# Lightning attention and a snake MLP in one kernel: squares taken off VectorE, matmuls without a reader, and a new program order

## Chip, core and metric

The kernel runs on one core of one Trainium2 chip. The metric is the device time of one launch in microseconds. Before the change the median of three runs is 239.01 us (238.47, 239.01 and 242.13).

The engines go by short names: PE is TensorE, DVE is VectorE, ACT is ScalarE, POOL is GpSimd, SP is SyncE, which here only issues transfers.

## The reference, cut to what matters

```python
# q, k, v: (4 batches, 8 heads, 768 positions, 64); lam: (8,)
for b in range(12):                                   # blocks of 64 positions
    intra = (qb @ kb.T * Dmask) @ vb                  # Dmask[i, j] = lam**(i-j) for i >= j
    inter = (qb * lam**(pos+1)) @ kv_state
    out[block] = intra + inter
    kv_state = lam**64 * kv_state + (kb * lam**(63-pos)).T @ vb

x = out.transpose(0, 2, 1, 3).reshape(3072, 512)      # tokens x model
h = x @ w_in                                          # 512 -> 2048
g = h + sin(alpha * h)**2 / (alpha + 1e-9)            # "snake"
y = g @ w_out                                         # 2048 -> 512
```

Inputs and output are float32. The kernel multiplies in bfloat16 and accumulates in float32.

## The kernel before

The work is cut into units and groups. A unit `u` is one batch, a window of 256 positions and four of the eight heads (24 units). Four units make a group `g` of 512 tokens (6 groups). Units run through attention, groups through the two layers of the MLP; both are interleaved.

Every engine takes its instructions strictly in the order of one string, `ORDER`. An item is `kind.indices:engine[:bank]`; the engine letters are T (PE), V (DVE), A (ACT), G (POOL) and S (SP), and the bank says which PSUM bank a matmul group uses. What an item waits for on other engines comes from its data, by semaphores. The kinds:

| kind | what it does |
|---|---|
| ld | load q, k or v of a unit (256 KB) |
| wi, wo | load a quarter of w_in or w_out, cast to bf16 by the transfer; issued by POOL |
| sq, sk, cv | scale q by lam^(pos+1), k by its reciprocal; cast v |
| tq, tk, tcq, tck | transpose q or k on PE, and copy the result out of PSUM |
| tdq, tdk | the same transposes by DMA (from unit 8 on) |
| s, m | scores on PE, and the causal mask on DVE |
| k, kc, a, n | k-v product on PE, its copy, the decayed state, the next state |
| o, x | attention output on PE, and its copy to bf16, the MLP's input |
| f1a, f1 | first layer, 128 of the 2048 columns: four matmuls of 512 tokens (f1a and f1: two halves of 256) |
| sin, sqr, stt | sine, its square, and h + square / alpha |
| f2 | second layer: a quarter of the sum for 128 tokens: four matmuls |
| oc, st | copy out of PSUM, store |
| lt, ltc | the last 128 tokens, in two halves of the columns |

A stretch of the order string, where the first squares stand:

```
... sin.0.0:A sin.0.1:A sin.0.2:A sqr.0.0:V f1a.0.3:T:5 f1.0.3:T kc.5:A tck.5:V sqr.0.1:G wi.2:G cv.6:V
k.6:T sqr.0.2:A sin.0.3:A tk.6:T:0 stt.0.0:V wi.3:G sq.7:V kc.6:A sqr.0.3:A tq.7:T:3 tck.6:A ...
```

The parts of the program that the change and the steps below touch (`...` marks cuts):

```python
    N0 = 28
    ...
    BANK = ("h0", "h1", "h2", "h3", "s0", "s1")
    def psum(shape, dtype, name, bank):
        return ps.tile(shape, dtype, name=name, tag=BANK[bank], bufs=1)
    ...
    def load_w_in(j, **_):                       # one quarter; POOL issues it
        w = DFF // WCH
        ld = nc.gpsimd.dma_start(out=w_in_sb[:, :, j * w:(j + 1) * w], in_=...)
        if j == 0:
            after(ld, loads[GATE])               # GATE = (3, 0): q of unit 3
    ...
    def scaled(u, j, name, bufs, tab, eng):      # sq, sk
        eng.tensor_tensor(out=t[:], in0=stage[u, j]..., in1=tab..., op=ALU.mult)
    ...
    def kv_decayed(u, c, eng, **_):              # a
        if prev is not None:
            eng.tensor_tensor(out=t[:], in0=x, in1=prev[:], op=ALU.add)      # kvx
        eng.tensor_tensor(out=kvbd[u, c][:], in0=x..., in1=LBD..., op=ALU.mult)
    ...
    def f1_part(g, f, bs):
        for c in range(NDC):                     # 4
            mlp[0] = nc.tensor.matmul(out=hps[g, f]..., lhsT=w_in_sb[:, c, f * P:(f + 1) * P],
                                      rhs=xt[g][:, c, bs]..., start=..., stop=...)
    def sine(g, f, **_):
        nc.scalar.activation(out=s1[g, f][:], in_=hps[g, f][:], func=ACTF.Sin,
                             scale=alpha_sb[:, f:f + 1])
    def square(g, f, eng, **_):
        if eng is nc.scalar:
            nc.scalar.activation(out=s2[g, f][:], in_=x[:], func=ACTF.Square)
        else:
            eng.tensor_tensor(out=s2[g, f][:], in0=x[:], in1=x[:], op=ALU.mult)
    def snake(g, f, **_):                        # stt; frees the PSUM bank of hps
        nc.vector.scalar_tensor_tensor(out=gall[g][:, f, :], in0=s2.pop((g, f))[:],
                                       scalar=r_sb[:, f:f + 1], in1=hps.pop((g, f))[:],
                                       op0=ALU.mult, op1=ALU.add)
    ...
    bz = ps.tile([P, 2 * P], FP32, name="bz", tag="h1", bufs=1)
    for _ in range(N0):                          # matmuls without a reader, at the start
        nc.tensor.matmul(out=bz[:], lhsT=zeros[:, :P], rhs=zeros[:], start=True, stop=True)
    ...
    for item in ORDER.split():
        name, eng, *bank = item.split(":")
        kind, *ix = name.split(".")
        DO[kind](*map(int, ix), eng=ENG[eng], bank=int(bank[0]) if bank else None)
```

Attention's PSUM tiles are `sp` in the banks s0 and s1 and `okv`, of which there is one.

Of the kernel before, what the change touches and what calls it, by code (L numbers as in the profile page):

```python
# [11 lines left out]
FP32 = mybir.dt.float32  # L12
# [6 lines left out]
ld.0.0:S ld.0.1:S sk.0:V sq.0:G tq.0:T:3 tk.0:T:0 ld.0.2:S ld.1.0:S ld.1.1:S ld.1.2:S ld.2.0:S  # L19
ld.2.1:S ld.2.2:S sk.1:G cv.0:V ld.3.0:S ld.3.1:S ld.3.2:S ld.4.0:S ld.4.1:S ld.4.2:S ld.5.0:S k.0:T  # L20
cv.1:G tcq.0:A tck.0:A tables:V sq.1:V s.0:T m.0.0:V kc.0:A m.0.1:V a.0.0:G k.1:T kc.1:A sq.2:V
sk.2:G sq.3:G sk.3:G ld.5.1:S ld.5.2:S ld.6.0:S ld.6.1:S ld.6.2:S ld.7.0:S ld.7.1:S ld.7.2:S
ld.8.0:S ld.8.1:S ld.8.2:S ld.9.0:S cv.2:A ld.9.1:S ld.9.2:S ld.10.0:S ld.10.1:S ld.10.2:S n.0.0:G
tq.1:T:3 tcq.1:V tk.1:T:2 tq.2:T:1 tck.1:V s.1:T m.1.0:V m.1.1:V tq.3:T:0 cv.3:A tcq.2:A o.0:T
tk.2:T:3 tck.2:A tk.3:T:2 a.1.0:V n.1.0:G s.2:T sq.4:V sk.4:V x.0.0:A o.1:T tck.3:V m.2.0:V m.2.1:V
x.1.0:A tcq.3:A k.2:T kc.2:V k.3:T cv.4:G sq.5:V kc.3:A tq.4:T:2 cv.5:A wi.0:G a.2.0:V s.3:T
tq.5:T:1 k.4:T kc.4:V tk.4:T:3 m.3.0:V m.3.1:V tck.4:A a.3.0:G sk.5:G o.2:T x.2.0:A a.4.0:V tcq.4:V
o.3:T a.1.1:V tcq.5:A x.3.0:A sq.6:G s.4:T tq.6:T:0 f1a.0.0:T:1 x.3.1:V tcq.6:A m.4.0:V n.4.0:V
sk.6:V f1.0.0:T tk.5:T:3 f1a.0.1:T:2 f1.0.1:T f1a.0.2:T:4 f1.0.2:T wi.1:G m.4.1:V n.1.1:G k.5:T
sin.0.0:A sin.0.1:A sin.0.2:A sqr.0.0:V f1a.0.3:T:5 f1.0.3:T kc.5:A tck.5:V sqr.0.1:G wi.2:G cv.6:V  # L30
k.6:T sqr.0.2:A sin.0.3:A tk.6:T:0 stt.0.0:V wi.3:G sq.7:V kc.6:A sqr.0.3:A tq.7:T:3 tck.6:A
stt.0.1:V stt.0.2:V sk.7:G stt.0.3:V f1.0.4:T:1 sin.0.4:A f1.0.5:T:2 n.3.0:V a.6.0:V tcq.7:A
sin.0.5:A o.4:T x.4.0:A s.5:T sqr.0.4:V stt.0.4:V tk.7:T:0 n.6.0:G f1.0.6:T:3 m.5.0:V m.5.1:V
tck.7:A cv.7:G k.7:T a.5.0:G sqr.0.5:G f1.0.7:T:1 sin.0.6:A kc.7:V s.6:T stt.0.5:V sqr.0.6:A
stt.0.6:V m.6.0:V m.6.1:V o.5:T f1.0.8:T:0 sin.0.7:A sqr.0.7:A sin.0.8:A f1.0.9:T:2 wo.0:G stt.0.7:V
a.7.0:G sqr.0.8:G f1.0.10:T:3 stt.0.8:V x.5.0:A wo.1:G sin.0.9:A sqr.0.9:A stt.0.9:V s.7:T o.6:T
m.7.0:V m.7.1:V f1.0.11:T:1 f1.0.12:T:0 sin.0.10:A sqr.0.10:A stt.0.10:V sin.0.11:A sqr.0.11:V
stt.0.11:V f1.0.13:T:2 f1.0.14:T:4 sin.0.12:A sqr.0.12:G n.5.0:V stt.0.12:V x.6.0:A sin.0.13:A o.7:T
sin.0.14:A x.7.0:A sqr.0.13:A sqr.0.14:A f1a.1.0:T:5 f1.0.15:T:3 f1.1.0:T sin.0.15:A a.0.1:G
stt.0.13:V sin.1.0:A stt.0.14:V sqr.0.15:V stt.0.15:V sk.8:G f1a.1.1:T:1 sqr.1.0:G stt.1.0:V  # L40
f1.1.1:T sin.1.1:A f1a.1.2:T:0 f1.1.2:T f1a.1.3:T:4 f1.1.3:T f1.1.4:T:2 sqr.1.1:G sin.1.2:A
sqr.1.2:V cv.8:G stt.1.1:V sin.1.3:A sqr.1.3:A sin.1.4:A stt.1.2:V f1.1.5:T:3 sin.1.5:A sqr.1.4:A
f1.1.6:T:5 sqr.1.5:A stt.1.3:V stt.1.4:V sin.1.6:A a.3.1:V k.8:T stt.1.5:V ld.11.0:S f1.1.7:T:1
cv.9:G sqr.1.6:A f1.1.8:T:4 f1.1.9:T:0 sin.1.7:A sqr.1.7:V n.0.1:V f1.1.10:T:2 sin.1.8:A sin.1.9:A
sqr.1.8:A sin.1.10:A stt.1.6:V wo.2:G stt.1.7:V sq.8:G f2.0.1.0:T:3 n.2.0:G a.2.1:G wo.3:G stt.1.8:V
f2.0.1.1:T f1.1.11:T:1 tdq.8:S ld.11.1:S ld.11.2:S cv.10:A sqr.1.9:A kc.8:A a.8.0:V sin.1.11:A
f2.0.1.2:T sk.9:G k.9:T sq.9:G n.3.1:V sq.10:G f2.0.0.0:T:4 sqr.1.10:V f2.0.0.1:T f2.0.0.2:T
f2.0.0.3:T oc.0.0:A kc.9:V tdk.8:S n.8.0:G sk.10:G sqr.1.11:V stt.1.9:V f2.0.2.0:T:0 f2.0.2.1:T
stt.1.10:V sq.11:G cv.11:A a.9.0:V a.5.1:V s.8:T n.2.1:G ld.12.0:S tdq.9:S tdk.9:S tdq.10:S m.8.0:V
tdq.11:S k.10:T f2.0.1.3:T m.8.1:V f1.1.12:T:2 n.7.0:V tdk.10:S kc.10:V s.9:T sk.11:G k.11:T  # L50
a.10.0:V sin.1.12:A st.0.0.0:S ld.12.1:S oc.0.1:V a.6.1:G f2.0.2.2:T f2.0.2.3:T a.7.1:G m.9.0:V
m.9.1:V kc.11:A sq.12:G o.8:T ld.12.2:S oc.0.2:V x.8.0:A s.10:T cv.12:A sqr.1.12:V m.10.0:V
f1.1.13:T:3 m.10.1:V n.9.0:G n.6.1:G n.5.1:V tdk.11:S o.9:T sin.1.13:A x.9.0:A f2.0.3.0:T:0
f2.0.3.1:T ld.13.0:S stt.1.11:V ld.13.1:S ld.13.2:S ld.14.0:S ld.14.1:S ld.14.2:S ld.15.0:S s.11:T
ld.15.1:S tdq.12:S n.10.0:V a.11.0:G sk.12:G o.10:T x.10.0:A sq.13:G stt.1.12:V f2.0.3.2:T tdq.13:S
f2.0.3.3:T sqr.1.13:G m.11.0:V m.11.1:V sq.14:G tdk.12:S sq.15:G stt.1.13:V ld.15.2:S ld.16.0:S
ld.16.1:S o.11:T x.11.0:V ld.16.2:S oc.0.3:V cv.13:A f1.1.14:T:1 f1.1.15:T:4 k.12:T sin.1.14:A
f1.2.0:T:5 f1.2.1:T:2 sqr.1.14:V stt.1.14:V sin.1.15:A sin.2.0:A a.4.1:G sk.13:G sqr.1.15:V
stt.1.15:V sqr.2.0:A stt.2.0:V sin.2.1:A f1.2.2:T:0 sin.2.2:A n.4.1:G a.9.1:G f1.2.3:T:3 n.11.0:V
sk.14:G n.7.1:G a.8.1:G f1.2.4:T:1 sin.2.3:A sqr.2.1:V stt.2.1:V sqr.2.2:A stt.2.2:V sin.2.4:A  # L60
sqr.2.3:V sqr.2.4:A tdq.14:S st.0.0.1:S tdq.15:S f1.2.5:T:4 kc.12:V f1.2.6:T:5 f1.2.7:T:0 sin.2.5:A
sin.2.6:A sin.2.7:A sqr.2.5:A stt.2.3:V stt.2.4:V sqr.2.6:V stt.2.5:V st.0.3.0:S tdk.13:S sqr.2.7:G
st.0.2.0:S f1.2.8:T:2 k.13:T f1.2.9:T:3 kc.13:A cv.14:A sin.2.8:A sqr.2.8:A stt.2.6:V f2.1.0.0:T:1
f2.1.0.1:T s.12:T sk.15:G stt.2.7:V k.14:T f1.2.10:T:0 tdk.14:S ld.17.0:S ld.17.1:S sin.2.9:A
f2.1.0.2:T sk.16:G n.8.1:G sqr.2.9:A kc.14:A m.12.0:V m.12.1:V a.12.0:G cv.15:G o.12:T ld.17.2:S
tdk.15:S n.9.1:G stt.2.8:V stt.2.9:V x.12.0:A s.13:T f1.2.11:T:2 a.10.1:G ld.18.0:S m.13.0:V
m.13.1:V k.15:T f2.1.0.3:T a.13.0:V kc.15:A oc.1.0:A s.14:T o.13:T sq.16:G sin.2.10:A cv.16:A
x.13.0:A f2.1.1.0:T:3 a.14.0:V m.14.0:V tdq.16:S st.0.1.0:S st.0.1.1:S sq.17:G sq.18:G tdq.17:S
m.14.1:V f1.2.12:T:1 s.15:T sin.2.11:A cv.17:A sqr.2.10:G a.15.0:V m.15.0:V stt.2.10:V o.14:T
x.14.0:A sin.2.12:A sqr.2.11:V sqr.2.12:V f2.1.1.1:T stt.2.11:V stt.2.12:V f2.1.1.2:T k.16:T  # L70
f1.2.13:T:4 sin.2.13:A n.12.0:V m.15.1:V f2.1.1.3:T sqr.2.13:V f1.2.14:T:0 sk.17:G stt.2.13:V
sin.2.14:A f1.2.15:T:2 tdk.16:S ld.18.1:S kc.16:V n.15.0:G sk.18:G s.16:T m.16.0:V o.15:T x.15.0:V
f2.1.2.0:T:1 oc.1.1:A f2.1.2.1:T sqr.2.14:V stt.2.14:V f1.3.0:T:3 sin.2.15:A sin.3.0:A ld.18.2:S
tdk.17:S f2.1.2.2:T k.17:T kc.17:A n.13.0:V f1.3.1:T:0 ld.19.0:S st.0.3.1:S a.11.1:G sqr.2.15:G
sin.3.1:A stt.2.15:V sqr.3.0:A m.16.1:V cv.18:G k.18:T s.17:T tdq.18:S tdk.18:S ld.19.1:S ld.19.2:S
ld.20.0:S st.0.2.1:S f2.1.2.3:T f2.1.3.0:T:2 f2.1.3.1:T cv.19:A sqr.3.1:G m.17.0:V stt.3.0:V
oc.1.2:V st.1.2.0:S sq.19:G tdq.19:S n.10.1:V m.17.1:V f1.3.2:T:3 f1.3.3:T:1 f2.1.3.2:T f2.1.3.3:T
kc.18:V a.16.0:V sk.19:G a.18.0:G n.11.1:G s.18:T stt.3.1:V o.16:T sin.3.2:A sqr.3.2:A m.18.0:V
sin.3.3:A oc.1.3:A sqr.3.3:A f1.3.4:T:0 x.16.0:V stt.3.2:V a.12.1:V sin.3.4:A sqr.3.4:A f1.3.5:T:4
stt.3.3:V ld.20.1:S ld.20.2:S ld.21.0:S ld.21.1:S stt.3.4:V a.17.0:V m.18.1:V f2.2.0.0:T:2  # L80
f2.2.0.1:T tdk.19:S f1.3.6:T:3 sin.3.5:A f1.3.7:T:0 k.19:T f1.3.8:T:5 sqr.3.5:V sin.3.6:A sqr.3.6:V
sin.3.7:A sqr.3.7:A stt.3.5:V sin.3.8:A st.1.0.0:S st.1.0.1:S st.1.3.0:S ld.21.2:S stt.3.6:V kc.19:V
st.1.1.0:S sqr.3.8:A ld.22.0:S ld.22.1:S f1.3.9:T:1 sin.3.9:A ld.22.2:S f2.2.0.2:T stt.3.7:V
f1.3.10:T:3 f1.3.11:T:0 stt.3.8:V sin.3.10:A st.1.3.1:S n.14.0:G sq.20:G s.19:T o.17:T a.14.1:V
f2.2.0.3:T sqr.3.9:G stt.3.9:V x.17.0:A f1.3.12:T:1 sqr.3.10:V o.18:T sk.20:G sk.21:G sin.3.11:A
oc.2.0:A a.19.0:V stt.3.10:V sq.21:G cv.20:G cv.21:G m.19.0:V f2.2.1.0:T:3 f1.3.13:T:2 f2.2.1.1:T
cv.22:G sin.3.12:A tdq.20:S st.2.0.0:S tdq.21:S sqr.3.11:V x.18.0:V sqr.3.12:A sin.3.13:A sqr.3.13:G
m.19.1:V stt.3.11:V stt.3.12:V a.15.1:G a.13.1:G n.15.1:V stt.3.13:V o.19:T f1.3.14:T:5 f1.3.15:T:4
f2.2.1.2:T x.19.0:A sin.3.14:A sin.3.15:A sq.22:G f2.2.1.3:T f2.2.2.0:T:0 f2.2.2.1:T f2.2.2.2:T
ld.23.0:S st.1.1.1:S sqr.3.14:G sqr.3.15:A st.2.0.1:S n.14.1:G tdk.20:S f1.4.0:T:1 sin.4.0:A  # L90
# [32 lines left out]
def kernel(  # L123
# [11 lines left out]
    nc = tc.nc  # L135
    P = nc.NUM_PARTITIONS
# [452 lines left out]
```

## Time and profile before

| | |
|---|---|
| time, median of three runs | 239.01 us |
| time of the profiled run | 243.51 us |
| its span, first to last instruction | 241.7 us |
| TensorE clock granted, mean | 0.932 |
| transfers | 33.92 MB, mean 140 GB/s |
| stores at the end: PE's last matmul to the end of the span | 236.2 to 241.7 us |

How to read it: the page's first part gives each engine's busy time, its share of the span and its instructions. The second part cuts the span into forty slices of 6.04 us; a digit is the busy share in tenths, and PEclk is the clock that TensorE was granted, in tenths of full speed. A table by stretch gives the same for stretches of one's choosing, in microseconds. A line of the waits reads: engine and line that waited, what it waited for, us in total, times, longest. A line in order of time reads: start, duration, engine, source line, operation, output and inputs. L452 is the first layer's matmul, L472 the sine, L481 the square on DVE or POOL, L479 the square on ACT, L486 the snake, L495 the second layer's matmul, L276 the scaling, L253 and L261 the loads of w_in and w_out. Matmuls overlap in the pipeline and their ends are modelled, so a busy PE does not mean that it works at its peak.

### The profile page before, as it was taken

Reading aid. Unit: us, or ns where it says so; the run is one execution under the profiler, and the core shown is the slowest. Engines: PE = TensorE matmul, PEld = TensorE weight load, DVE = VectorE, ACT = ScalarE, POOL = GpSimd, SP = SyncE. Lnnn points to the kernel's source line nnn. Section 1 sums busy time; section 2 is a strip of 40 time slices with the busy share of each in tenths; the row PEclk is TensorE's granted clock in tenths of the full one; section 3 lists DMA queues with packets and bytes.
Section 4 is the critical chain, followed back from the end, with each engine's and each line's share of the span. In section 5 each row is a group of like instructions: output and inputs, shape, how many; then the busy total and the mean of one; then the engine's idle time right before and its main releaser. Section 6 shows DMA issues by size and latency. Waiting matters only on the chain.

```text
span 241.7 us, 5272 instructions
## 1 busy us (share of the span) xinstructions
PE 216.5 (90%) x2049; PEld 112.1 (46%) x2077; DVE 166.2 (69%) x290; ACT 119.1 (49%) x207; POOL 110.3 (46%) x148
## 2 busy tenths in 40 slices
PE   8487599699959999998999997999999999999990
PEld 5354375246414554454444444444445444444460
DVE  2977758598996998989967999347676645664100
ACT  2244349489841336956535565427763255544010
POOL 5756237338955667797339046941532101111000
PEclk9955569799979999999999999999999999999998
DMA  5999979990898999984863994404811200305314
GB/s 147 292 290 248 247 198 198 221 170 5 131 163 161 191 291 200 193 195 93 215 178 90 224 232 108 90 0 91 188 32 43 60 8 0 87 1 113 87 23 109
DMA packets 63850, 33.92 MB, mean 140 GB/s; under 512 B 19648, under 2 KB 60880, under 8 KB 63824
## 3 DMA queue, kind: packets, MB, share of 16 engines
q1 hardware_dynamic: 59344, 29.31, 54.0%
q0 software_dynamic: 4224, 4.19, 11.0%
q8 instruction: 16, 0.26, 0.5%
q10 hardware_dynamic: 256, 0.08, 0.1%
q14 instruction: 10, 0.08, 0.1%
HBM read 27.28 MB, written 6.29 MB: 139 GB/s over the span
## 4 chain that ended last, share of the span: by engine, by line
PE 65%; DVE 9%; DMA 7%; issue 6%; ACT 4%; SPq 4%; POOL 2%; ACTq 0%; POOLq 0%
PE ops L495 31%; PE hps L452 25%; SPq L243 4%; DMA w_in_sb<-in_moe_w_in_dram 4%; DMA st_k<-in_k_dram 3%; ACT s L472 2%; DVE gall L486 2%; PE sp L344 2%; DVE s L481 2%; PE okv L429 2%; PE okv L420 2%; PE okv L375 1%; PE ops L518 1%; DVE ST L354 1%; DVE kvbd L397 1%
## 5 line engine op out<-in xcount | busy, mean ns | idle before, releaser
L452 PE MATMUL hps<-xt,w_in_sb 128*128 128x512 bf16 (+1 forms) x403 | 94.4, 379 | 7.4 <-DMA w_in_sb<-in_moe_w_in_dram 3.7
L472 ACT ACTIVATE s<-hps,alpha_sb 128x512 bf16<-128x512 f32 x96 | 64.9, 688 | 59.5 <-PE hps L452 50.5
L495 PE MATMUL ops<-w_out_sb,gall 128*128 128x512 bf16 x353 | 84.7, 381 | 2.8 <-DVE gall L486 1.3
L486 DVE SCALAR_TENSOR_TENSOR gall<-s,r_sb,hps 128x512 bf16<-128x512 bf16 x96 | 69.6, 742 | 22.7 <-POOL s L481 12.4
L481 POOL TENSOR_TENSOR s<-s 128x512 bf16<-128x512 bf16 x25 | 26.3, 1054 | 81.5 <-ACT s L472 72.1
L452 PEld LDWEIGHTS <-w_in_sb 128*128 128x128 bf16 x416 | 40.4, 102 | 48.0 <-issue 6.1
L495 PEld LDWEIGHTS <-gall 128*128 128x128 bf16 x368 | 34.9, 98 | 42.9 <-issue 2.4
L354 DVE TENSOR_TENSOR ST<-sp,mask 128x512 bf16<-128x512 f32 x48 | 31.3, 682 | 9.9 <-PE sp L344 9.7
L481 DVE TENSOR_TENSOR s<-s 128x512 bf16<-128x512 bf16 x33 | 20.5, 621 | 11.0 <-ACT s L472 10.9
L276 POOL TENSOR_TENSOR KD<-st_k,R 128x512 bf16<-128x512 f32 x21 | 23.0, 1101 | 5.4 <-PE hps L452 3.9
L479 ACT ACTIVATE s<-s 128x512 bf16<-128x512 bf16 x38 | 23.6, 630 | 0.9 <-DVE gall L486 0.3
L276 POOL TENSOR_TENSOR QL<-st_q,E 128x512 bf16<-128x512 f32 x19 | 20.4, 1075 | 4.2 <-DMA st_q<-in_q_dram 3.8
L267 ACT COPY ob<-ops 128x512 f32<-128x512 f32 (+1 forms) x16 | 8.9, 557 | 24.8 <-PE ops L495 22.3
L267 ACT CAST xt<-okv 128x512 bf16<-128x512 f32 (+1 forms) x18 | 10.4, 577 | 14.1 <-PE okv L429 14.1
L344 PE MATMUL sp<-QT 64*64 64x128 bf16 x384 | 11.5, 235 | 1.7 <-DVE ST L354 0.7
L397 DVE TENSOR_TENSOR kvbd<-kvx,LBD 128x256 bf16<-128x256 f32 x17 | 11.4, 669 | 0.6
L344 PEld LDWEIGHTS <-QT 64*64 64x64 bf16 x384 | 7.5, 115 | 8.3 <-issue 6.2
L429 PE MATMUL okv<-ST,VB 64*64 64x128 bf16 x384 | 10.9, 237 | 0.0
L375 PE MATMUL okv<-VB,KD 64*64 64x64 bf16 x320 | 7.9, 205 | 3.2 <-POOL VB L269 1.5
L269 DVE COPY ob<-ops 128x512 f32<-128x512 f32 x9 | 6.1, 683 | 6.6 <-PE ops L495 6.6
L267 ACT COPY QT<-pt 128x512 bf16<-128x512 bf16 x11 | 6.5, 598 | 7.6 <-PE pt L303 7.6
L375 PEld LDWEIGHTS <-KD 64*64 64x64 bf16 x320 | 5.7, 115 | 9.6 <-issue 7.3
(59 smaller groups left out, 147.3 us busy)
## 6 DMA issues: line engine op xcount, KB each, us to landing
st_q<-in_q_dram SPq DMA_DIRECT2D x24, 256.0 KB, 5.2
st_k<-in_k_dram SPq DMA_DIRECT2D x24, 256.0 KB, 5.0
st_v<-in_v_dram SPq DMA_DIRECT2D x24, 256.0 KB, 5.2
out_dram<-ob SPq DMA_DIRECT2D x46, 128.0 KB, 2.4
w_in_sb<-in_moe_w_in_dram POOLq DMA_DIRECT2D x4, 512.0 KB, 9.6
w_out_sb<-in_moe_w_out_dram POOLq DMA_DIRECT2D x4, 512.0 KB, 8.5
QT<-QL SPq DMA_TRANSPOSE x16, 3.1
QT<-KD SPq DMA_TRANSPOSE x16, 3.2
```

The source lines that it names most:

```text
L267: nc.scalar.copy(out=out, in_=in_)
L276: eng.tensor_tensor(out=t[:], in0=stage[u, j][:].rearrange("p h two e -> p two h e"), in1=tab[:, :, hh * HH:(hh + 1) * HH].unsqueeze(3).to ...
L344: nc.tensor.matmul(out=sp[hd][half[c], par, hp, :], lhsT=QT[half[hd], 1, par, hp, half[c]], rhs=QT[half[hd], 0, :, hp, half[c]], start=Tru ...
L354: nc.vector.tensor_tensor(out=stm[u][:, hd], in0=sps[u][hd][:], in1=mask[:].unsqueeze(2).to_broadcast([P, 2, 2, P]), op=ALU.mult)
L375: nc.tensor.matmul(out=okv[u][half[hd], c, 2 * P + hp * D:2 * P + (hp + 1) * D], lhsT=KD[half[c], par, h, :], rhs=VB[half[c], par, h, :], ...
L429: nc.tensor.matmul(out=okv[u][half[hd], c, hp * P:(hp + 1) * P], lhsT=VB[half[c], par, 2 * hp + hd, :], rhs=ST[half[c], hd, par, hp, :], s ...
L452: mlp[0] = nc.tensor.matmul(out=hps[g, f][:].rearrange("p (b i) -> p b i", b=2)[:, bs] .rearrange("p b i -> p (b i)"), lhsT=w_in_sb[:, c, ...
L472: nc.scalar.activation(out=s1[g, f][:], in_=hps[g, f][:], func=ACTF.Sin, scale=alpha_sb[:, f:f + 1])
L479: nc.scalar.activation(out=s2[g, f][:], in_=x[:], func=ACTF.Square)
L481: eng.tensor_tensor(out=s2[g, f][:], in0=x[:], in1=x[:], op=ALU.mult)
L486: nc.vector.scalar_tensor_tensor(out=gall[g][:, f, :], in0=s2.pop((g, f))[:], scalar=r_sb[:, f:f + 1], in1=hps.pop((g, f))[:], op0=ALU.mul ...
L495: mlp[0] = nc.tensor.matmul(out=ops[g, m][:], lhsT=gall[g][:, f, m * P:(m + 1) * P], rhs=w_out_sb[:, f, :], start=(f == 0), stop=(f == NFC ...
```

## The change

Three things are done at once. The squares of group 1 and later no longer run on DVE, only on ACT and POOL (group 0 keeps four). Nine groups of matmuls without a reader are put among PE's items of the first stages; they multiply a tile of zeros by itself into a PSUM bank that nothing reads, and are meant to keep TensorE from being idle while it waits for data. And the whole order string is a new one: other interleaving, other engines for many of the small operations, other banks. What is computed stays the same.

| items by engine | before | after |
|---|---|---|
| sqr | DVE 33, ACT 38, POOL 25 | DVE 4, ACT 60, POOL 32 |
| a (decayed state) | DVE 21, POOL 19 | DVE 7, POOL 33 |
| n (next state) | DVE 15, POOL 17 | DVE 5, POOL 27 |
| sq, sk (scaling) | DVE 8, POOL 40 | DVE 4, POOL 44 |
| cv | DVE 2, ACT 12, POOL 10 | DVE 0, ACT 13, POOL 11 |
| kc | DVE 10, ACT 14 | DVE 13, ACT 11 |
| tcq, tck | DVE 5, ACT 11 | DVE 8, ACT 8 |
| x | DVE 7, ACT 18 | DVE 10, ACT 15 |
| oc | DVE 9, ACT 14 | DVE 11, ACT 12 |
| w (matmuls without a reader) | 0 | 9 items, 36 matmuls |

The order of POOL's items up to the last quarter of w_in:

```
before: sq.0 sk.1 cv.1 a.0.0 sk.2 sq.3 sk.3 n.0.0 n.1.0 cv.4 wi.0 a.3.0 sk.5 sq.6 wi.1 n.1.1 sqr.0.1 wi.2 wi.3
after:  sq.0 sk.1 cv.1 sq.2 sk.2 a.0.0 cv.3 sk.3 wi.0 sq.4 a.3.0 a.2.0 sk.5 wi.1 n.0.0 sq.5 a.0.1 a.4.0 cv.5
        sq.6 wi.2 sk.6 cv.6 n.2.0 sq.7 n.1.1 n.4.0 wi.3
```

The diff, its core (the order string is cut to its first lines):

```diff
 ORDER = """
-ld.0.0:S ld.0.1:S sk.0:V sq.0:G tq.0:T:3 tk.0:T:0 ld.0.2:S ld.1.0:S ld.1.1:S ld.1.2:S ld.2.0:S
-ld.2.1:S ld.2.2:S sk.1:G cv.0:V ld.3.0:S ld.3.1:S ld.3.2:S ld.4.0:S ld.4.1:S ld.4.2:S ld.5.0:S k.0:T
-...
+ld.0.0:S ld.0.1:S ld.0.2:S ld.1.0:S ld.1.1:S ld.1.2:S ld.2.0:S ld.2.1:S ld.2.2:S ld.3.0:S sq.0:G
+ld.3.1:S ld.3.2:S ld.4.0:S ld.4.1:S tq.0:T:2 sk.0:V tk.0:T:0 sq.1:V cv.0:A sk.1:G tables:V k.0:T
+cv.1:G sq.2:G tq.1:T:3 kc.0:V tcq.1:V sk.2:G w.5:T:h1 tk.1:T:1 tck.1:A k.1:T tcq.0:V tck.0:V s.0:T
+m.0.0:V a.0.0:G m.0.1:V kc.1:V tq.2:T:0 w.4:T:h2 tk.2:T:2 cv.2:A k.2:T kc.2:A tck.2:A s.1:T ld.4.2:S
+...
@@
+    def warm_up(n, tag):
+        shape = [P, 2, 512] if tag == "okv" else [P, 512]
+        t = ps.tile(shape, FP32, name="bz", tag=tag, bufs=1)
+        t = t[:, 0] if tag == "okv" else t[:]
+        for _ in range(n):
+            nc.tensor.matmul(out=t[:, :2 * P], lhsT=zeros[:, :P], rhs=zeros[:],
+                             start=True, stop=True)
+
     for item in ORDER.split():
         name, eng, *bank = item.split(":")
         kind, *ix = name.split(".")
+        if kind == "w":
+            warm_up(int(ix[0]), bank[0])
+            continue
         DO[kind](*map(int, ix), eng=ENG[eng], bank=int(bank[0]) if bank else None)
```

## Prediction, made before the result was known

> **What bounds the kernel now.** I read the page first: engine shares, then the forty slices, then the chain that ended last; after that the tables by stretch, the waits, and the time order of single engines. The page's first part names the engine:
>
> ```profile
> PE 216.5 (90%) x2049; PEld 112.1 (46%) x2077; DVE 166.2 (69%) x290; ACT 119.1 (49%) x207; POOL 110.3 (46%) x148
> ...
> PE   8487599699959999998999997999999999999990
> ...
> PEclk9955569799979999999999999999999999999998
> ```
>
> TensorE (PE) is nearly always busy, but busy is not work done. The PEclk row says that slices 3 to 5 (12 to 30 us, a slice being 6.04 us) ran at half clock, with lesser dips later. So I count work instead. In the chain, eight matmuls of 512 columns take 1.73 us at full clock: 0.216 us each, 0.863 us for a block of four. Sixteen score matmuls take 0.35 us, and so on; all that the program lists for PE comes to 198 us. The span is 241.7 us. Where the other 44 us lie, the table by stretch shows (columns: us, PE, PEld, DVE, ACT, POOL busy, clock, DMA share, GB/s):
>
> ```profile
> 0.00:30.00 30.00, 20.00 (x314) 14.07 (x315) 20.62 (x50) 10.74 (x20) 16.30 (x30) 0.68 1.03 245
> 30.00:60.00 30.00, 27.96 (x297) 16.35 (x300) 21.57 (x36) 21.78 (x39) 15.23 (x20) 0.86 0.82 161
> 60.00:93.00 33.00, 29.48 (x326) 14.04 (x330) 29.03 (x47) 14.73 (x28) 22.42 (x30) 0.95 1.05 181
> 93.00:140.00 47.00, 45.01 (x457) 21.69 (x464) 40.76 (x72) 28.08 (x50) 28.68 (x39) 1.00 0.78 180
> 140.00:190.00 50.00, 48.07 (x420) 23.43 (x427) 34.97 (x58) 25.60 (x45) 22.42 (x26) 1.00 0.38 88
> ```
>
> The first matmul of group 2's first layer starts at 93.1 us. By count 138.4 us of PE work stand after it; they end at 236.2 us, after 143.1. So behind 93 us only 4.7 us are lost, and the last copy and store add 5.5. **The loss lies ahead of 93 us**: 59.4 us of work took 93.1. There are three stages. Up to 29 us, data: the DMA share is above 1. From 29 to 73 us, two waits and three stretches of half clock. From 60 to 93 us, VectorE (DVE) is busy 29.03 of 33 us. The waits of PE, longest first:
>
> ```profile
> PE hps L452 <- DMA w_in_sb<-in_moe_w_in_dram: 3.7, 2, 1.9
> PE hps L452 <- DVE gall L486: 2.9, 1, 2.9
> ```
>
> The first is two waits of 1.9 and 1.8 us for quarters of w_in, at 29.1 and 44.7 us. The second, at 69.6 us, is the most telling: a first-layer matmul wants a PSUM bank that a DVE `snake` has not yet freed. The time order of DVE and of GpSimd (POOL) there says why:
>
> ```profile
> 64.05 3.98 DVE L481 TENSOR_TENSOR s<-s 128x512 bf16<-128x512 bf16 x1
> 67.95 0.28 DVE L405 TENSOR_TENSOR kvs<-kvx,LHP 128x128 f32<-128x128 f32 x1
> 68.15 2.05 DVE L486 SCALAR_TENSOR_TENSOR gall<-s,r_sb,hps 128x512 bf16<-128x512 bf16 x3
> ```
>
> ```profile
> 63.87 0.80 POOL L261 DMA_DIRECT2D w_out_sb<-in_moe_w_out_dram  x1
> 64.69 1.05 POOL L276 TENSOR_TENSOR KD<-st_k,R 128x512 bf16<-128x512 f32 x1
> 65.70 2.04 POOL L276 TENSOR_TENSOR QL<-st_q,E 128x512 bf16<-128x512 f32 x2
> ```
>
> One DVE square took 3.98 us, where the median of the 33 is 0.425 and their mean 0.621, and it ended when a run of POOL work ended (67.7 us). After the PE pause the clock is 0.50 until about 72.3 us.
>
> **What the Trainium skill says.** "SBUF — State Buffer", section "Who interferes with whom", says that a VectorE instruction with two SBUF inputs contends with a GpSimd instruction that reads SBUF, that the loser is blocked, and that one with a single SBUF input is left alone. The trace agrees: the square (both inputs in SBUF) stretched to 3.98 us, while `snake` (one input from PSUM) keeps 0.742 us on the mean. "GPSIMD Engine Reference", section "4.1 Engine selection", puts a two-input elementwise operation at about twice VectorE's time; here it is 1.054 us on POOL against 0.425 undisturbed, 2.5 times. "TensorE: Matmul & The Clock Gate", section "What's actually happening", says that PE runs at half clock until it has been busy for a window of some 3.4 us, and falls back after an idle one. The trace agrees after the pauses; but between 12 and 28 us PE is busy by record 11.7 of 16 us (the 2 us stretches, added) and the clock stays at 0.50. So small matmuls do not seem to count as activity.
>
> **The change, part by part.**
>
> Squares. They were 33 on DVE, 38 on ScalarE (ACT), 25 on POOL; they become 4, 60, 32. Off DVE: 29 × 0.621 = 18.0 us. On ACT: 22 × 0.630 = +13.9. On POOL: 7 × 1.054 = +7.4.
>
> Other placement in the new order. DVE gives up 14 decayed states (about 1.17 us each, kvx 0.497 and kvbd 0.669), 10 state updates (0.42) and 4 scalings (0.95), and takes back a few copies. Summed by rows of the page, DVE's list falls from 179 to 144 us (overlapping starts make the list's sum larger than the 166 busy), ACT's rises from 128 to 137, POOL's from 110 to 141. Up to the last `snake` of group 1 the gain is small: 52.8 us of DVE list from the first `snake` on become 47.9. But seven of the squares that can be blocked leave group 1.
>
> Weights. This is a matter of order alone, and I think it is the largest part. Quarter 0 of w_in goes out at 19.57 us now, behind the cast of v for unit 4. In the new order it stands behind the scaled k of unit 3: v of unit 3 is there at 15.0 us, cast 0.7 and scaling 1.04 make 16.8; with the 9.6 us to landing of the page, 26.4 us against 29.1. Quarter 2 now stands behind a POOL square and goes out at 34.98 us, and the wait at 44.7 us is for it. In the new order it follows quarter 1 (about 22.5 us, once k of unit 5 is scaled) by six POOL operations, 5.0 us: out at 27.5, there at 37. Quarter 3 follows after another 5.0 us: there at 42.
>
> Matmuls without a reader. 36, of 256 columns. The trace's 28 of the same shape took 4.73 us, so 36 take 6.1 us. They lie ahead of the second layer's start, most of them before 26 us, where PE waits for data anyway; I put at most 1 us of them on the path. Their use would be to hold the clock.
>
> Sum, in the stages of the profiled run: first layer starts sooner, 2.7 us; wait for quarter 2 with its cold stretch (1.8 us, and half of the 3.7 us at 0.50 after it, 1.85), 3.6; DVE pause and its cold stretch (2.9 and half of 2.7), 4.2; part of the cold start at 29 to 34.8 us (half of 5.7 is 2.9), take 1.2; fewer small stalls behind 93 us, 1.5. That is 13.2 us. Given back: a wait for quarter 1, due at about 32 us when PE could take it at 30.2 (26.4 and 3.8 of work), 1.5; the unread matmuls, 1. That leaves about 11.5.
>
> One correction: the profiled run took 243.5 us, the median is 239.0. Some of the cold stretches and waits that I count must be missing in the median run, so I take off 4.5: 7 us. **239.0 − 7 = 232.0 us.**
>
> **Rivals.** (1) POOL becomes the bound. It goes to some 141 us of list, takes its work strictly in order, and a square behind two scalings waits 2 us, and with it `snake` and the bank. For it: in 60 to 93 us POOL is already busy 22.4 of 33. Against it: POOL spends 72.1 us waiting for sines ahead of squares, so it has room, and in group 1 just one square is left to it. If it held, stalls of 1 to 2 us per group would leave 237 to 241. (2) DMA is the bound up to 93 us, so earlier weights only push q, k, v back. For it: share 1.03 and 1.05 in the first and third stretch. Against it: between 54 and 62 us the share is under 0.06, because the transposes stand behind a POOL scaling issued at 61.2; in the new order that scaling comes some 15 us sooner. It would make 235 to 238. (3) The clock stays at half in spite of the extra matmuls: that loses only my 1.2 us. If instead it stays full from 12 us on, gain another 2 to 3, so 229.
>
> **Range and chances.** The floor is firm: 138.4 us of work behind group 2's start, 5.5 of tail, 1.8 between span and time. Group 2's start at 78.5 us (26.4 and 52.1 of work) without one stall gives 224. Rivals 1 and 2 together reach 239. I take 226 to 238, faster by over 2% (below 234.2) 0.66, within 2% 0.28, slower 0.06.
>
> **What would show it.** Right: first-layer matmuls begin at 26 to 27 us; no wait for w_in near 45; no DVE square of several us and no pause near 67; group 2's first layer at 80 to 85 us; DVE busy near 135 us, POOL near 140, ACT near 130. Wrong: waits of `snake` on POOL squares that grow from 12.4 us, half clock after 40 us, or a start of group 2 later than 88 us.

## The result, and the profile after

The changed kernel takes 230.98 us (median of four runs, 228.56 to 233.56) against 240.57 for the kernel before in the same count of runs: 0.959 of it, 95% interval 0.9504 to 0.9676. (The runs of a kernel fall into a faster and a slower group; ratios and intervals compare the faster runs alone, so they differ a little from the ratio of the medians, which count all runs.) Repeated later beside other variants it came out at 0.9629 (0.9577 to 0.9682). The prediction was 232.0 us, with a range of 226 to 238.

The page of the changed kernel, its engine shares and the rows of PE and of its clock:

```profile
PE 211.3 (93%) x2081; PEld 110.3 (49%) x2111; DVE 139.2 (61%) x231; ACT 126.3 (56%) x219; POOL 135.5 (60%) x195
...
PE   8587877999999999989999999999999999999993
...
PEclk9969999999999999999999999999999999999999
```

The half clock of 12 to 30 us has shrunk to one dip, and DVE has lost 27 us of work. The table by stretch, cut near the new start of group 2's first layer (columns as before the change):

```profile
0.00:30.00 30.00, 24.00 (x387) 17.11 (x387) 22.11 (x46) 11.28 (x21) 22.93 (x40) 0.94 1.06 251
30.00:60.00 30.00, 27.49 (x297) 14.92 (x302) 25.14 (x42) 25.93 (x45) 21.21 (x28) 1.00 0.93 175
60.00:80.00 20.00, 19.84 (x253) 9.85 (x258) 16.29 (x28) 12.07 (x23) 12.36 (x20) 1.00 1.15 234
80.00:127.00 47.00, 45.20 (x470) 22.07 (x476) 31.63 (x50) 31.49 (x57) 40.53 (x63) 1.00 1.06 221
```

PE's longest waits for a snake and for w_in:

```profile
PE hps L453 <- DVE gall L487: 0.9, 3, 0.5
...
PE hps L453 <- DMA w_in_sb<-in_moe_w_in_dram: 0.5, 1, 0.5
```

Where 2.9 and 3.7 us stood, 0.9 and 0.5 are left. These source lines are one further down than in the kernel before (L453 for L452, L487 for L486), since the order string is one line longer. In PE's order of time group 2's first layer starts here (five blocks at once):

```profile
82.31 4.49 PE L453 MATMUL hps<-xt,w_in_sb 128*128 128x512 bf16 x20
```

Against the 93.1 us of the prediction's table this looks like 10.8 us. But the profiled run of the kernel before took 243.51 us, 4.5 more than the median. A copy of it with two items moved, which by time is the same (ratio 1.001, below), was profiled at 239.51 us, and I compare stages with that one:

```profile
89.26 7.72 PE L452 MATMUL hps<-xt,w_in_sb 128*128 128x512 bf16 x35 [0.16 <-issue]
```

Three other kernels of the old order, each with one edit (below: squares alone, w_in alone, unread matmuls alone), start group 2 at 88.2 to 88.5 us. So ahead of group 2's start the gain is 6 to 7 us; from there to the start of PE's last item it is about 2, 139.3 to 136.9 (137.5 in the repeated run). Together that is 8 to 9 us; the medians differ by 9.6.

### The profile page after: what moved, and what is told of

It is laid out like the page before. It is cut to its first block, busy times and chain, and to the rows that moved or that the text cites. A ratio compares the mean times of both kernels' runs of the same rounds, so it can differ in the third digit from the quotient of the medians.

```text
span 226.8 us, 5334 instructions
## 1 busy us (share of the span) xinstructions
PE 211.3 (93%) x2081; PEld 110.3 (49%) x2111; DVE 139.2 (61%) x231; ACT 126.3 (56%) x219; POOL 135.5 (60%) x195
## 3 DMA queue, kind: packets, MB, share of 16 engines
q0 software_dynamic: 4224, 4.19, 11.5%
## 4 chain that ended last, share of the span: by engine, by line
PE 77%; DVE 9%; DMA 4%; POOL 3%; issue 2%; ACT 2%; SPq 1%; DVEq 0%; ACTq 0%; POOLq 0%
PE ops L496 33%; PE hps L453 31%; PE okv L430 3%; PE sp L345 3%; DMA QT<-KD 2%; PE okv L421 2%; PE okv L376 2%; DVE gall L487 2%; DMA lam_bc<-in_lam_dram 2%; PE ops L519 2%; DVE kvx L394 1%; PE bz L563 1%; DVE ST L355 1%; DVE kvbd L398 1%; POOL QL L277 1%
## 5 line engine op out<-in xcount | busy, mean ns | idle before, releaser
L487 DVE SCALAR_TENSOR_TENSOR gall<-s,r_sb,hps 128x512 bf16<-128x512 bf16 x96 | 69.4, 743 | 41.7 <-POOL s L482 23.0
L453 PE MATMUL hps<-xt,w_in_sb 128*128 128x512 bf16 (+1 forms) x399 | 89.9, 362 | 2.2 <-DVE gall L487 0.9
L482 POOL TENSOR_TENSOR s<-s 128x512 bf16<-128x512 bf16 x32 | 33.1, 1041 | 45.0 <-ACT s L473 44.8
L453 PEld LDWEIGHTS <-w_in_sb 128*128 128x128 bf16 x416 | 38.7, 98 | 41.4 <-issue 1.2
L355 DVE TENSOR_TENSOR ST<-sp,mask 128x512 bf16<-128x512 f32 x48 | 31.5, 683 | 13.6 <-PE sp L345 13.5
L480 ACT ACTIVATE s<-s 128x512 bf16<-128x512 bf16 x60 | 36.6, 626 | 1.2 <-DVE gall L487 0.4
L277 POOL TENSOR_TENSOR QL<-st_q,E 128x512 bf16<-128x512 f32 x22 | 22.9, 1044 | 0.4 <-DVE E L217 0.3
L398 POOL TENSOR_TENSOR kvbd<-kvx,LBD 128x256 bf16<-128x256 f32 x26 | 16.1, 619 | 2.0
L268 ACT CAST xt<-okv 128x512 bf16<-128x512 f32 (+1 forms) x15 | 8.5, 568 | 13.6 <-PE okv L430 11.6
L270 DVE COPY ob<-ops 128x512 f32<-128x512 f32 x11 | 7.5, 685 | 13.2 <-PE ops L496 13.1
L394 POOL TENSOR_TENSOR kvx<-kva,kvs 128x128 f32<-128x128 f32 x26 | 12.2, 468 | 3.8 <-DVE kva L270 2.0
L268 ACT CAST VB<-st_v 128x512 bf16<-128x512 f32 x13 | 8.0, 615 | 6.7 <-DMA st_v<-in_v_dram 6.7
L270 POOL CAST VB<-st_v 128x512 bf16<-128x512 f32 x11 | 6.7, 612 | 3.7 <-DMA st_v<-in_v_dram 3.7
```

What stands on the lines that cost most here:

```text
L268: nc.scalar.copy(out=out, in_=in_)
L277: eng.tensor_tensor(out=t[:], in0=stage[u, j][:].rearrange("p h two e -> p two h e"), in1=tab[:, :, hh * HH:(hh + 1) * HH].unsqueeze(3).to ...
L355: nc.vector.tensor_tensor(out=stm[u][:, hd], in0=sps[u][hd][:], in1=mask[:].unsqueeze(2).to_broadcast([P, 2, 2, P]), op=ALU.mult)
L398: eng.tensor_tensor(out=kvbd[u, c][:], in0=x.unsqueeze(2).to_broadcast([P, 2, 2, D]), in1=LBD[:, 2 * hh:2 * hh + 2, :].unsqueeze(3).to_bro ...
L453: mlp[0] = nc.tensor.matmul(out=hps[g, f][:].rearrange("p (b i) -> p b i", b=2)[:, bs] .rearrange("p b i -> p (b i)"), lhsT=w_in_sb[:, c, ...
```

## The experiments

Every kernel keeps the whole computation. The edits are to the order string; ratios are to the kernel before.

**Without the unread matmuls.**

```diff
-... sk.2:G w.5:T:h1 tk.1:T:1 ...      (nine items w.*)
+... sk.2:G tk.1:T:1 ...
```

> The changed kernel without its nine groups of unread matmuls; all else the same. My theory: before 26 us TensorE waits for data, so the clock there hardly matters, and the new order and the free VectorE keep it busy afterwards: the time rises by at most 1.5 us over the changed kernel's (median 231.0), the first-layer matmuls begin at 25.6 us as before, and the half clock ends within some 4 us of their start. Rival (the unread matmuls carry a large part of the gain): half clock from 11 to beyond 33 us, the first layer of group 0 runs at half speed, group 2 starts 3 us or more later than 82.3 us, and the time is 234 to 237.

Measured: 227.86 us, 0.9538 (0.9471 to 0.9605). Its clock row and its first matmuls of the first layer:

```profile
PEclk9955599999999999999999999999999999999999
```

```profile
26.07 2.74 PE L452 MATMUL hps<-xt,w_in_sb 128*128 128x256 bf16 x12
```

The half clock is back for three slices, and twelve matmuls that took 1.59 us in the changed kernel take 2.74. In the trace it costs nothing: the first layer starts at 26.07 us instead of 25.59, and group 2 at 82.26 instead of 82.31. The rival is out. So is my allowance of a small use: the median is 3 us lower without them. Since the intervals of 0.9538 and of the repeated 0.9629 overlap, I call it "no gain, probably a loss".

**The squares alone, in the old order.**

```diff
-sqr.1.2:V  sqr.1.7:V  ... sqr.5.15:V      (29 items)
+sqr.1.2:A  sqr.1.7:A  ... sqr.5.15:A      (engine as in the changed kernel)
```

> The kernel before, its order untouched, only the 29 VectorE squares of groups 1 to 5 given to ScalarE or GpSimd as the change does. My theory: the blocked square at 64 us goes, and with it the pause of 2.9 us and the half clock behind it: 3 to 4.5 us faster than before, with the w_in wait at 44.7 us still there. Rival (VectorE was not the limit, the order was): within 1.5 us of before, the pause near 67 us comes back from a ScalarE or GpSimd square that is late.

Measured: 241.68 us, 1.0117 (1.0044 to 1.019): 1.2% slower. My theory fell. DVE where the blocked square had stood:

```profile
60.98 0.73 DVE L486 SCALAR_TENSOR_TENSOR gall<-s,r_sb,hps 128x512 bf16<-128x512 bf16 x1
61.64 3.10 DVE L405 TENSOR_TENSOR kvs<-kvx,LHP 128x128 f32<-128x128 f32 x1
64.66 2.05 DVE L486 SCALAR_TENSOR_TENSOR gall<-s,r_sb,hps 128x512 bf16<-128x512 bf16 x3
```

The square is gone, and the next DVE operation with two SBUF inputs, a state update that takes 0.28 us undisturbed, is blocked for 3.10 us in its stead, to the end of the same POOL run. PE still pauses 2.29 us; that is not the rival's reason either, since no late square is in it. Behind it, ACT squares come late for group 2: PE waits for snakes at 93, 95 and 98 us, and from group 2's start on the kernel is 2.4 us slower than in the old order (141.7 against 139.3).

**w_in's quarters 2 and 3 early, in the old order.**

```diff
-... sq.6 wi.1 n.1.1 sqr.0.1 wi.2 wi.3     (POOL's items)
+... sq.6 wi.1 wi.2 n.1.1 wi.3 sqr.0.1
```

> The kernel before, only with quarters 2 and 3 of w_in issued ahead of GpSimd's first square instead of behind it. My theory: out at 25 to 27 us instead of 35, landed by 37 to 40; the wait for w_in at 44.7 us and its half clock are gone, group 0 ends 2 to 3.5 us sooner; but VectorE is the limit behind it, so of that only 1 to 3 us remain in the time. Rival (transfers are the bound): the earlier quarters push q, k and v of units 6 to 8 back by as much, and the time is the same within 1 us.

Measured: 238.4 us, 0.9938 (0.990 to 0.9976). The quarters go out at 25 and 26.6 us, but block 8 of group 0, the first that needs quarter 2, starts at 42.9 us, and with the quarters late (the copy with two items moved) at 42.1 without a wait for them. The wait of 1.8 us at 44.7 us that the prediction read is in the profile of 243.51 us alone; no other trace of the old order has it, so there was no such wait to remove; what the 0.6% come from stays open. The first layer started later in this trace, at 30.1 us instead of 28.6, after a wait of 2.65 us for quarter 0 (1.2 us there). The two loads behind it may have slowed that quarter, as the rival has it; one trace does not show it.

**The squares back on DVE, in the new order.** The 29 items again, the other way.

> The changed kernel with the same 29 squares put back on VectorE, in the new order. My theory: VectorE has room in the new order (139 of 227 us busy), so what costs is blocking by GpSimd, which is busier now: some squares of 1 to 4 us, one or two pauses of TensorE; 1.5 to 4 us slower than the changed kernel (231.0). Rival (the order alone makes the gain): within 1 us of the changed kernel.

Measured: 231.22 us, 0.9701 (0.961 to 0.9791). The ratio is 0.7 to 1.1% above the changed kernel's 0.9629 and 0.959, with overlapping intervals; the median is 0.2 us above the changed kernel's first and 0.1 below its second. The longest DVE square is 2.06 us, so blocking is there. The trace does not settle it: its run is the slowest of the four (233.83 us), and group 2 starts 3.1 us later in it; 2.2 of these are lost by 39.5 us, ahead of every square that was moved. What moving the squares is worth in the new order stays open, from nothing to some 2%.

**The two blocked items moved, in the old order.**

```diff
-sqr.1.7:V  n.0.1:V
+sqr.1.7:A  n.0.1:G
```

> The kernel before with two items moved off VectorE and nothing else: the square that was blocked for 3.98 us (group 1, item 7) to ScalarE, and the next VectorE operation with two SBUF inputs behind it (the next state of unit 0, which took 3.10 us in the run with all squares moved) to GpSimd. My theory now: a run of GpSimd operations blocks whichever VectorE operation with two SBUF inputs comes first, and with both gone none stands in that stretch: no VectorE operation above 1.5 us between 58 and 68 us, the pause of TensorE near 66 us under 0.6 us, time 1.5 to 4 us faster than before. Rival (the pause comes from late squares, whoever makes them): the pause stays above 1.5 us and the time is within 1 us of before.

Measured: 239.46 us, 1.0012 (0.9978 to 1.0046). The blocking is gone: DVE runs three snakes from 58.95 us on in 2.20 us. The time does not move. PE's waits, longest first:

```profile
PE ops L495 <- DMA w_out_sb<-in_moe_w_out_dram: 3.1, 1, 3.1
```

Once PE no longer pauses for a snake, it arrives at the last quarter of w_out before that has landed (issued at 60.0 us, awaited until 70.1). My expectation had the pause right and the time wrong: in this trace a wait of the same length stands behind the pause.

**w_out early as well.**

```diff
-... wo.1 sqr.0.12 ... cv.9 n.0.1 wo.2 sq.8 n.2.0 a.2.1 wo.3 sk.9 ...
+... wo.1 wo.2 wo.3 sqr.0.12 ... cv.9 n.0.1 sq.8 n.2.0 a.2.1 sk.9 ...
```

> The kernel before with the two VectorE items moved (as in the run where the blocking was gone and a wait of 3.1 us for the last quarter of w_out stood in its place), and quarters 2 and 3 of w_out issued right behind quarter 1, at 46 to 48 us instead of 56.5 and 60. Theory (the blocking and the late w_out stood side by side, each hiding the other): with both gone no pause of TensorE above 1 us between 60 and 75 us, group 2's first layer starts at 85 to 87 us instead of 89.3, time 2 to 3.5 us (0.8 to 1.5%) faster than before. Rival (transfers are full there, so the earlier w_out pushes back q, k, v or the transposes of units 8 to 11): group 2 starts within 1 us of 89.3, the time is the same within 1 us, and TensorE waits for another transfer.

Measured: 236.03 us, 0.9885 (0.9855 to 0.9915), group 2 at 85.39 us. Both signs as the theory has them.

**w_out early alone.** The same move, the two DVE items left in place.

> The kernel before with quarters 2 and 3 of w_out issued behind quarter 1 and nothing else: the fourth corner beside before, the two moved VectorE items alone (1.001 of before) and both together (0.9885). Theory (the blocking and the late w_out stand side by side and each hides the other): the blocked square of group 1 is still there with its pause of TensorE of 2 to 3 us, and the time is within 0.5% of before. Rival (the late w_out alone was the loss, the moved items add nothing): 0.985 to 0.992 of before, as with both.

Measured: 235.98 us, 0.9803 (0.9748 to 0.9859). Here the rival is right: moving w_out is enough. The two medians, 235.98 and 236.03, are the same; the ratios differ because each was taken beside other runs of the kernel before (medians 240.15 and 239.11). So w_out alone is worth 1.2 to 2%. DVE, and below it POOL, where the blocked square had stood:

```profile
62.00 0.55 DVE L481 TENSOR_TENSOR s<-s 128x512 bf16<-128x512 bf16 x1
62.47 1.13 DVE L405 TENSOR_TENSOR kvs<-kvx,LHP 128x128 f32<-128x128 f32 x1
63.52 2.05 DVE L486 SCALAR_TENSOR_TENSOR gall<-s,r_sb,hps 128x512 bf16<-128x512 bf16 x3
```

```profile
61.05 1.22 POOL L276 TENSOR_TENSOR KD<-st_k,R 128x512 bf16<-128x512 f32 x1
62.23 2.27 POOL L276 TENSOR_TENSOR QL<-st_q,E 128x512 bf16<-128x512 f32 x2
```

The same square meets the same three scalings, now with no issue of a quarter ahead of them, and takes 0.55 us; the state update behind it takes 1.13, both inside the run. The scalings take a little longer (1.22 and 2.27 us against 1.05 and 2.04), and PE's pause shrinks from 2.9 to 0.34 us. One edit thus removed both waits; why DVE gets through here is not shown. The "each hides the other" of my expectation holds in one direction only: moving the DVE items did nothing without w_out. (Group 2 starts at 87.08 us in this trace, later than the 85.39 above: another DVE square, at 38 us, was blocked for 1.83 us, and PE waited 1.8 us behind it.)

**All of w_in early too, in the old order.** The kernel with w_out early and the two items moved, and:

```diff
-... sk.3 n.0.0 n.1.0 cv.4 wi.0 ... wi.1 n.1.1 sqr.0.1 wi.2 wi.3
+... sk.3 wi.0 n.0.0 n.1.0 cv.4 ... wi.1 wi.2 n.1.1 wi.3 sqr.0.1
```

> The same, and all four quarters of w_in early as well: quarter 0 right behind the scaling of unit 3's k (15.5 us instead of 19.7), quarters 2 and 3 ahead of GpSimd's first square. Theory (the new order's gain ahead of group 2 is mostly the weights' places in GpSimd's order): first layer at 25.5 to 27 us instead of 28.6, group 2 at 82.5 to 85 us, time 4.5 to 7 us (2 to 3%) faster than before, so that over half of the changed kernel's gain is reached in the old order. Rival (it is the whole interleaving that counts, not a few items): at most 1.2% faster, with VectorE or a late q, k, v holding group 0 to within 1.5 us of where it was.

Measured: 233.01 us, 0.9765 (0.9716 to 0.9814). Group 2's start in PE's order of time:

```profile
82.92 7.29 PE L452 MATMUL hps<-xt,w_in_sb 128*128 128x512 bf16 x33 [0.16 <-issue]
```

82.92 us against the changed kernel's 82.31. With seven items moved in an order of a thousand, five of them weight loads, nearly all that the change gains ahead of group 2 is there. The first layer starts at 27.49 us, later than I expected; 0.9765 is about three fifths of the changed kernel's gain (2.35 of 3.7 to 4.1%). What remains lies behind group 2: 138.7 us against 136.9.

The changed kernel itself has w_in about as early (out at 16.6 to 32.0 us, with the seven moves at 15.6 to 28.2), but not w_out:

```profile
51.67 0.79 POOL L262 DMA_DIRECT2D w_out_sb<-in_moe_w_out_dram  x1
...
55.35 0.80 POOL L262 DMA_DIRECT2D w_out_sb<-in_moe_w_out_dram  x1
```

These are its quarters 2 and 3; with the seven moves they are out by 45.1 us. The changed kernel has no wait for w_out all the same: PE first uses the last quarter at 63.6 us. So the seven moves show what the weights' places are worth in the old order. That the changed kernel gains its 6 to 7 us in the same way is likely for w_in and not shown for w_out; no run puts the weights back to late places in the new order.

**Unread matmuls in the old order.** 36 of them, in about the changed kernel's places.

> The kernel before with 36 unread matmuls put among TensorE's items of the first stages, in about the places that the change has, and nothing else. My theory: the clock is full from about 16 us on, but the first layer still waits for w_in at 29 us and again near 44 us; the first layer of group 0 then runs 2.9 us quicker and waits that much longer for quarter 2: the time is within 1 us of before. Rival (the clock was the loss): 2.5 to 4 us faster.

Measured: 239.06 us, 0.9952 (0.9914 to 0.9991). The clock is at 0.984 on the mean, and the first layer still starts at 29.19 us, behind w_in. The ratio is worth 1.2 us, a little more than the 1 us of my theory and under half of the rival's least. The second wait, for quarter 2, is not in this trace either: block 8 starts at 41.66 us without one.

**The changed kernel again, and one blocked item moved.**

> The changed kernel once more, beside its variants on the same chip: 229 to 232, 3.5 to 4.5% under the kernel before; the run without unread matmuls (227.9) then lies 0.5 to 1.3% below it.

Measured: 231.35 us, 0.9629 (0.9577 to 0.9682). DVE and POOL in the changed kernel, where the blocking survives:

```profile
27.85 3.12 DVE L394 TENSOR_TENSOR kvx<-kva,kvs 128x128 f32<-128x128 f32 x1
31.01 0.42 DVE L398 TENSOR_TENSOR kvbd<-kvx,LBD 128x256 bf16<-128x256 f32 x1
```

```profile
27.87 1.05 POOL L277 TENSOR_TENSOR KD<-st_k,R 128x512 bf16<-128x512 f32 x1
28.86 0.62 POOL L270 CAST VB<-st_v 128x512 bf16<-128x512 f32 x1
29.43 0.40 POOL L406 TENSOR_TENSOR kvs<-kva,LHP 128x128 f32<-128x128 f32 x1
29.79 1.03 POOL L277 TENSOR_TENSOR QL<-st_q,E 128x512 bf16<-128x512 f32 x1
```

A 0.3 us addition lasts 3.12 us, until the POOL run of four ends. So, without the unread matmuls:

```diff
-a.1.1:V
+a.1.1:G
```

> The changed kernel without the unread matmuls, and with the decayed state of unit 1, chunk 1, on GpSimd instead of VectorE: in the changed kernel its first operation was blocked for 3.12 us at 27.9 us, in the run without unread matmuls for 1.88 us at 29.7 us. My theory: VectorE is free some 2 us sooner at 31.5 us, the pauses of TensorE at 32 to 35 us for snakes go, GpSimd's quarter 3 goes out 1.1 us later and is still in time; 0.5 to 2 us faster than without unread matmuls alone (227.9), so 226 to 227.4. Rival (the transfers of the first 37 us are the bound): the same within 0.5 us.

Measured: 228.14 us, 0.9505 (0.9456 to 0.9553). The pauses at 32 to 35 us are gone and group 2 starts at 80.47 us. Against the run without unread matmuls (0.9538, median 227.86) the time does not resolve it, which is the rival's figure, though the trace (226.57 us, the fastest of its six runs) shows the stage shorter. Against the changed kernel the intervals don't touch: with both edits, this is the fastest version by ratio, and it beats both kernels.

**The other decayed state of unit 1 moved too.**

```diff
-a.1.0:V
+a.1.0:G
```

> The changed kernel without unread matmuls, with both decayed states of unit 1 on GpSimd (the run with one of them moved: 228.1 median, 0.9505 of before). VectorE's first of them was blocked for 1.86 us at 17.1 us in the changed kernel. Theory (blocking falls on the next operation with two SBUF inputs): the scaling of unit 4's k, next on VectorE, is blocked in its stead, so the first layer starts within 0.5 us of 26.0 and the time is the same within 0.7 us. Rival (one blocked operation less is one less): first layer 1 us sooner and 0.7 to 1.5 us faster.

Measured: 228.22 us, 0.955 (0.9502 to 0.9597): no further gain, as the theory has it, but not for its reason. In the run with one decayed state moved, the one compared with, it was the next scaling on DVE, at 17.3 us, that was blocked, for 2.89 us; now it takes 1.07, and the first layer starts at 25.21 us instead of 26.03, outside the theory's 0.5 us and near the rival's 1. What was gained is lost behind it: the half clock ends 1.9 us later in this trace (29.75 us against 27.83), a square at 33.6 us takes 1.64, and group 2 starts at 81.99 us instead of 80.47.

## Why the prediction was right, point by point

*Where the loss lay.* Right: 6 to 7 of 8 to 9 us came from ahead of group 2's start, which the prediction put at 80 to 85 us and which came at 82.3.

*First layer sooner, 2.7 us.* Right, and by the reason given: PE no longer waits for quarter 0. Quarter 0 went out at 16.61 us (16.8 predicted), quarters 1, 2 and 3 at 21.60, 27.06 and 32.00 (22.5, 27.5, 32.5), and the first layer began at 25.59 (26.4), 3.0 us before the old order's 28.57.

*Wait for quarter 2 with its cold stretch, 3.6 us.* Wrong. It stands in no other trace of the old order, and early quarters 2 and 3 alone gave 0.6%. The 4.5 us taken off for "some of the cold stretches and waits that I count must be missing" is about the size of this term, without knowing which it was.

*DVE pause with its cold stretch, 4.2 us, from the squares.* The pause went, but the step from squares to pause failed. Squares taken off DVE alone made the old order slower (1.0117), the blocking passed to the next two-input operation, and once that was moved too, a wait of 3.1 us for w_out stood in the place. The term's size was about right, 4.2 us against the 2.7 to 4.7 that early w_out brings, and its cause was not: in the old order what pays is the place of w_out in POOL's order (0.9803 alone, 0.9885 with the two items moved), of which the prediction did not speak.

*Clock, 1.2 us gained and 1 us given back for the unread matmuls.* They do raise the clock. In the old order that brings about what the term says (0.9952, between 0.1 and 0.9%), in the new order nothing: the first layer runs 1.2 us faster there and PE then waits for quarter 1 and for snakes (0.5 us each and less), so that group 2 starts at the same time. Rival 3's "gain another 2 to 3" fell with it.

*Given back for quarter 1, 1.5 us.* The wait is there and shorter: 0.5 us, 0.9 in the repeated run.

*Fewer stalls behind 93 us, 1.5 us.* Right in size, about 2 us. Its cause is not settled: putting the squares back in the new order loses it in the trace (139.05 us from group 2 to the last item), but part of that is waits for DMA transposes, and the medians show no difference.

*Busy times, 135, 140 and 130 us.* Measured 139.2, 135.5 and 126.3. The sign that I named for failure, snakes waiting longer for POOL squares, came (12.4 to 23.0 us) and is not passed on: PE's own waits for snakes fell from 2.9 to 0.9 us. With that rival 1 (POOL as the bound, 237 to 241 us) is out, and so is the time that rival 2 (DMA, 235 to 238) forecast.

The sum itself has a slip: 13.2 less 1.5 and 1 is 10.7, not 11.5, so by its own terms the forecast was 232.8 us. And the total was right partly by luck, because a correction that named no cause took out about as much as the wrong terms had put in. What the runs show: in the old order, places of weight loads in POOL's order give about three fifths of the gain; an unexplained 2 us of the interleaving lie behind group 2. Of the two things that head the change's description, the squares made the old order slower and are worth nothing to 2% in the new one, and the unread matmuls are probably a loss there.

## What to carry to other kernels

Look at where weight loads stand in the order of the engine that issues them: a load queued behind an operation that waits for a late result is late for no other reason, as w_in's quarters 2 and 3 were behind a square (out at 35.0 us and later, at 25 and 26.6 ahead of it). Before crediting a pause with its length, ask what would end next; a wait of equal length may stand behind it. And when an operation is blocked by a neighbour, look at the neighbour's run: moving the victim can hand the wait to the next one in line, as it did with the squares.

## What the runs showed of the hardware

A DVE operation with two SBUF inputs that meets a run of POOL operations can last until the run ends, not until one POOL operation ends: 3.98, 3.12 and 3.10 us in three kernels, for operations of 0.43, 0.28 and 0.28 us. The Trainium skill's "SBUF — State Buffer", section "Who interferes with whom", states the contention for an instruction; these traces show whole runs of three or four. It is no rule: in the kernel with w_out early alone two DVE operations came through inside the run in 0.55 and 1.13 us, and in the kernel with two items moved a square took 1.26 us (from 65.1 us) inside a run of two scalings. What decides is not shown.

The clock of PE does not go by busy time alone. In the kernel before, PE was busy by record for the whole stretch from 21.2 to 24.6 us, with small attention matmuls, and the clock stayed at 0.50; from 69.0 to 72.4 us it was busy for 2.80 of 3.40 us, with matmuls of 512 columns, and the clock rose to full at the end. With the 36 unread matmuls (128 rows, 128 columns of weights, 256 of data) the clock was full from 15.1 us on in the new order and from 14.5 in the old. That suggests that small matmuls count for less. It is not a clean rule either: in the run with the squares moved in the old order, 3.45 of 3.50 us of small matmuls, from 13.6 to 17.1 us, were followed by 3.4 us at full clock.

Why the changed kernel's time is nevertheless higher with the unread matmuls stays open: in the profiled runs group 2 starts at the same time, and 1.1 us are lost behind it, with a wait of 0.9 us for a DMA transpose at 100 us that the other run doesn't have. The rest of the 3 us lies in runs whose traces were not kept: the profiled repeat took 229.24 us at a mean clock of 0.991, its five companions 230.07 to 232.25 us at 0.975 to 0.977.
